# One more drain of GpSimd behind the writes of the last pair but one, in a linear-attention and mixture-of-experts kernel

## The chip, the core and the metric

The kernel runs on one core of a Trainium2 chip. A core has five engines with queues of their own: TensorE (PE in the profile, its weight loads PEld), VectorE (DVE), ScalarE (ACT), GpSimd (POOL) and SyncE (SP). They wait for each other through semaphores. Data moves between the chip's memory and the core by DMA, issued here by SP, by ACT, and, where the rows are picked by a list of indices, by POOL.

The metric is the time of one execution on the device in microseconds (us), as the median of several runs.

## What is computed

Lightning attention over 4 batches, 8 heads, 768 positions and 64 features per head, in blocks of 64 positions, and then a mixture of experts over the 3072 rows of 512 that come out of it. The second part, which the change is about, does this for each row:

```python
for s in range(S):
    fresh_e = int(np.argmax(logits[b, s]))
    if s == 0 or local_gate[b, s] < 0.5:
        e = fresh_e
    else:
        e = prev_e if prev_e >= 0 else fresh_e
    prev_e = e
    ls = logits[b, s] - logits[b, s].max()
    p = np.exp(ls)
    p /= p.sum() + 1e-09
    h = np.maximum(x[b, s] @ w1[e], 0.0)
    out[b, s] = p[e] * (h @ w2[e])
```

There are 8 experts with w1 of 512 x 1024 and w2 of 1024 x 512. Which expert a row goes to is known only while the kernel runs.

## The kernel before

The attention runs first, in 24 steps of 128 positions of one batch. Its rows are written to a buffer in the chip's memory, x_dram. From the logits the kernel works out, on the core itself, tiles of 128 rows that share an expert, and for each slot of a tile the index of its row. A tile is then brought in by an indirect DMA of POOL (`collect`, L725, a gather from x_dram), multiplied by the expert's two weight matrices on TensorE, scaled by the gate, and written by an indirect DMA of POOL to its rows of the output (`scatter`, L768, or `write_pair`, L776).

The first tiles go one by one (L899 to L945). Most of the rest go in pairs of tiles that share an expert (`pair`, L1004). `pair(p)` brings the rows of pair p + 2 and prepares pair p + 1 while it multiplies pair p. How many pairs there are depends on the routing: `rest` (L1272) runs pair 3 and then, by nested branches in `later_pairs` (L1285), as many more as the number `more` says. With these inputs four more run, pairs 4 to 7. Each is a call of `later_pair(k, last)` (L1279). It first writes the result of the pair before it, from the tile `yt`, with `write_pair`: two indirect writes, i = 0 and 1, of 128 rows each, whose indices lie in the small tile `sidxp`. Then it runs its own pair. So when the last pair, 7, begins, pair 6, the last but one, is written. The result of pair 7 goes to another tile (`yl`, which lies in the memory of `s1`, so that the profile calls it s), and is written by the last statement of the kernel, `write_pair(yl)` (L1318).

What sets the order: PE, DVE, SP and ACT run in the order of the code in this part (L1209). POOL's order is left to the scheduler of the framework, within the dependencies. Each engine takes its instructions in turn, and an instruction that waits holds up those behind it on the same engine. The writes to the output don't wait for each other (`apart`, L763). At each join of two branches the framework adds steps that bring the semaphores of the paths to the same counts; POOL's are INC_SWDGE_SEM in the profile and carry the line of the branch or of the end of the program.

The framework closes the program at L1359: SP waits until every DMA has landed, each engine drains, all five meet at a semaphore, POOL clears the semaphores, and they meet again. A drain is an instruction that ends when the engine has finished what was issued to it before.

Of the kernel before, what the change touches and what calls it, by code (L numbers as in the profile page):

```python
# [29 lines left out]
N = B * S  # L30
# [35 lines left out]
def kernel(  # L66
# [9 lines left out]
    nc = tc.nc  # L76
# [313 lines left out]
    sidxp = route.tile([P, 2], U32, name="sidxp")  # L390
# [271 lines left out]
    def rows_out(i):  # L662

        got = nows["got"]
        nc.vector.tensor_scalar(got[:, 0], got[:, 0], 0.0, float(SKIP), ALU.is_equal, ALU.mult)
        nc.vector.tensor_tensor(sidx[i], got[:, 0], gidx[i], ALU.add)

    def both_halves():

        twin = pl[:, :5 * (E + 1)].rearrange("p (k g) -> p k g", k=5)  # L670
        few = nows["few"]
        nc.tensor.matmul(twin[:, :, :E], lhsT=dupb, rhs=few, start=True, stop=True, skip_group_check=True)
        nc.tensor.matmul(twin[:, :, E:], lhsT=dupq, rhs=few[:, :, 0:1], start=True, stop=True, skip_group_check=True)
        got = act.tile([P, 5, E + 1], F32, name="twin", bufs=1)
        nc.vector.tensor_copy(got, twin)
        src = act.tile([P, 2, E + 1], F32, name="srch", bufs=1)
        nc.vector.tensor_scalar(src[:, 0], got[:, 0], -float(P), 0.0, ALU.add, ALU.max)
        nc.vector.tensor_scalar(src[:, 1], got[:, 0], 0.0, float(SKIP), ALU.is_equal, ALU.mult)
        nc.vector.tensor_tensor(src[:, 0], src[:, 0], src[:, 1], ALU.add)
        nc.vector.tensor_tensor(src[:, 0], src[:, 0], got[:, 1], ALU.add)  # L680
        nc.vector.scalar_tensor_tensor(sidxh[:, :E], src[:, 0, :E], 2.0, upper.broadcast_to([P, E]), ALU.mult, ALU.add)
        nc.vector.scalar_tensor_tensor(sidxh[:, E:], src[:, 0, E:], 4.0, fourth, ALU.mult, ALU.add)
        nc.vector.tensor_tensor(got[:, 2], got[:, 2], got[:, 3], ALU.add)
        nc.vector.tensor_tensor(gateh, got[:, 2], got[:, 4], ALU.add)
# [21 lines left out]
    def weights_of(g, i, layers=(1, 2), cond=None, own=None):  # L706
        e = expert(g, own)
        if 1 in layers:
            nc.sync.dma_start(out=w1t[i], in_=w1_src(e), cond=cond, cond_hint=None if cond is None else True)
        if 2 in layers:  # L710
            nc.sync.dma_start(out=w2t[i], in_=w2_src(e), cond=cond, cond_hint=None if cond is None else True)

    def w_of(p):
        return (p + 1) % 2
# [48 lines left out]
    def apart(rows):  # L763

        tc.declare_no_dep(rows.ins, group="out", reason="no row is written twice")
        tc.add_to_no_dep_group("out", rows.ins)
# [9 lines left out]
    def write_pair(y):  # L776

        for i in range(2):
            apart(nc.gpsimd.indirect_dma_start(out=out, out_offset=bass.IndirectOffsetOnAxis(ap=sidxp[:, i:i + 1], axis=0),
                                               in_=y[:, i], in_offset=None, bounds_check=N - 1, oob_is_err=False))  # L780

    def gate_of(g):
        i, j = at(g)
# [6 lines left out]
    def number(k, n):  # L790
        return nc.values_load(arms[k][0:1, 0:1], min_val=0, max_val=n - 1,
                              skip_runtime_bounds_check_because="a number of tiles")
# [15 lines left out]
    with tc.manual_schedule(engines={PE, DVE, SP, POOL}):  # L808
# [71 lines left out]
        yt = act.tile([P, 2, DM], F32, name="y", bufs=1)  # L880
# [70 lines left out]
    def xp(p, j):  # L951
        return xps[2] if j else xps[p % 2]
# [16 lines left out]
    def sums_1(p, ns):  # L969
        fs = sums(s1, a1(p, 0, 0), a1(p, 0, 1), a1(p, 1, 0), a1(p, 1, 1), True)  # L970
        for n in ns:
            fs[n]()
# [21 lines left out]
    def pair_ahead(p):  # L994
        for i in range(2):
            ahead(KA + 2 * p + i, i)

    def pair_flipped(i):
        flipped(xqs[i], xgt[i])

    def pair_moved(p, i):
        moved(xp(p, i), xqs[i])
# [106 lines left out]
    def ahead_half(h):  # L1109
        collect(xgh, 1, G2 - KA + h)  # L1110
# [98 lines left out]
    with tc.manual_schedule(engines={PE, DVE, SP, ACTE}):  # L1209
        more, fulls, halves = (number(k, n) for k, n in enumerate((PMAX - PMIN + 1, E + 1, FIRST_SMALL + 1)))  # L1210
        weights_of(KA, w_of(0), (2,))
        weights_of(G2, 2)
        both_halves()
        pair_ahead(0)
        rows_out(1)
        ahead_half(0)
        sums_1(0, range(3))
        pair_flipped(0)
        pair_flipped(1)
        hidden(0, 0, 0)  # L1220
        hidden(0, 0, 1)
        pair_moved(0, 0)
        moved(xp(0, 1), xqs[1], copy=nc.vector.tensor_copy)
        sums_1(0, (3,))
        output(0, 0)
        sums_of_x(0)
        pair_ahead(1)
        written(4, 0)

        def first_pairs(n, first=2):  # L1230
            hooks = hooks_of_halves(n, first)

            def loads():
                nc.vector.tensor_copy(owner[2], owner[1])
                weights_of(KA + 2, w_of(1), own=2)

            hooks.setdefault(1, []).insert(0, loads)
            pair(0, hooks)
            pair(1, {k - 14: f for k, f in hooks.items()})

        def others():
            weights_of(G1, 2)
            rows = [xgh, *xgt]

            def full_ahead(f):
                collect(rows[f % 3], *at(G1 + f))

            pair(2, {0: [lambda: full_ahead(0)], 10: [lambda: full_ahead(1)], 12: [lambda: full_ahead(2)],
                     6: [lambda: flipped(xqs[0], rows[0])], 7: [lambda: moved(xtt[0], xqs[0])]}, load=False, further=False)

            def w_of_full(f):
                return w_of(2) if f % 2 else 2

            def full(f, n=E):

                i, w = f % 2, w_of_full(f)
                if f + 3 < n:
                    full_ahead(f + 3)
                if not f:
                    weights_of(G1 + 1, w_of_full(1), cond=fulls > 1)  # L1260
                if f + 1 < n:
                    flipped(xqs[1 - i], rows[(f + 1) % 3])
                hidden(i, w, 0)
                hidden(i, w, 1)
                if f + 1 < n:
                    moved(xtt[1 - i], xqs[1 - i])
                output(i, w)
                written(G1 + f, i)
                if f + 2 < n:
                    weights_of(G1 + f + 2, w, cond=fulls > f + 2)  # L1270

            def rest(asked=False):  # L1272
                if not asked:
                    pair_ahead(4)
                weights_of(KA + 8, w_of(4), cond=more > 0)
                rows_of_pair(3)
                pair(3, cond=more > 1, write=False)

                def later_pair(k, last):  # L1279

                    write_pair(yt)
                    pair(PMIN + k, {11: [lambda: rows_of_pair(PMIN + k)]}, next=not last, load=not last and PMIN + k + 2 < PMAX,
                         cond=more > k + 2, write=False)

                def later_pairs(k):  # L1285

                    if PMIN + k + 1 == PMAX:
                        return later_pair(k, True)
                    with tc.If(more > k + 1, preferred_fallthrough_block=True) as cmp:
                        later_pair(k, False)  # L1290
                        later_pairs(k + 1)
                    with cmp.Else():
                        later_pair(k, True)

                with tc.If(more > 0, preferred_fallthrough_block=True) as cmp:
                    later_pairs(0)
                with cmp.Else():
                    for i in range(2):
                        nc.vector.tensor_copy(yl[:, i], yt[:, i])

            with tc.If(fulls == 3, preferred_fallthrough_block=True) as cmp:
                for f in range(3):
                    full(f, 3)
                    if f:
                        ahead(KA + 7 + f, f - 1)
                rest(True)
            with cmp.Else():
                while_more(fulls, 0, E, None, full)
                rest()


        with tc.If(halves == FIRST_SMALL, preferred_fallthrough_block=True, label="halves") as cmp:
            first_pairs(3, 4)
            others()
        with cmp.Else():
            one_of(halves, [3, 4, 2, 5, 1, 6, 0, 7, 8], None, first_pairs)
            others()
        write_pair(yl)  # L1318


# [42 lines left out]
```

## Time and profile before

| what | us |
|---|---|
| median of 3 runs | 442.13 |
| the runs | 440.86, 442.13, 446.67 |
| the profiled execution, its own time | 443.53 |
| its span, first to last instruction | 441.8 |
| PE busy in it | 426.0 |
| POOL busy in it | 109.2 |
| indirect transfers issued by POOL (each about 1.0 us on POOL) | 29 gathers, 27 writes |

The profile is one execution, taken by the hardware profiler. Its times are counted from the first instruction of the span. A row of a group has the line of the kernel, the engine (a q behind it marks its queue: steps that wait, branch or issue and don't count as busy), the operation, the tiles written and read, the count and the times. L1359 is the closing of the program, L779 the indirect write in `write_pair`, L1289 the branch in `later_pairs`. The chain of waits is followed back from the last instruction, at each step to what released it. The granted TensorE clock was 0.996 of full speed on average.

### The profile page before, as it was taken

The page shows a single profiled execution, that of the slowest core. Times are in us where ns is not written, and L with a number is a line of the kernel's source. Part 1 is how long each engine was busy: PE and PEld are TensorE (multiplying, and loading weights), DVE is VectorE, ACT ScalarE, POOL GpSimd, SP SyncE. Part 2 cuts the span into 40 slices and gives each one's busy share as a digit, 9 for nine tenths or more (in the row PEclk, how much of TensorE's full clock was granted, in tenths as well). Part 3 has the DMA queues.
Part 4 walks back from the last instruction along what each step waited for, and adds up shares of the span by engine and source line. Part 5 has one row for each costly group of instructions (what it writes and reads, how often), then busy time and mean ns, then how long its engine had stood idle before and what let it go on. Part 6 is the DMA issues. An engine that isn't in the chain of part 4 may idle for free.

```text
span 441.8 us, 10324 instructions
## 1 busy us (share of the span) xinstructions
PE 426.0 (96%) x4094; PEld 354.7 (80%) x4094; DVE 283.5 (64%) x552; ACT 195.1 (44%) x591; POOL 109.2 (25%) x120
## 2 busy tenths in 40 slices
PE   7998979999999999999999999999999999999993
PEld 7787767787766886977867999667999999898982
DVE  5767886954249868857463784100687879878661
ACT  4245546446455106564234555451555454565110
POOL 4483674430100032114211302100202020020101
PEclk9999999999999999999999999999999999999998
DMA  8999999999999899999993799996165828370101
GB/s 263 412 363 350 329 371 330 330 384 337 370 391 400 300 311 393 401 396 404 395 398 126 266 401 367 336 352 218 40 216 159 310 78 303 122 269 3 55 1 52
DMA packets 48351, 124.84 MB, mean 283 GB/s; under 512 B 3164, under 2 KB 10844, under 8 KB 46368
## 3 DMA queue, kind: packets, MB, share of 16 engines
q1 hardware_dynamic: 42624, 108.03, 66.7%
q0 software_dynamic: 4368, 13.90, 9.0%
q10 hardware_dynamic: 1296, 2.10, 1.3%
q8 instruction: 36, 0.59, 0.5%
q14 instruction: 27, 0.22, 0.1%
HBM read 124.02 MB, written 12.91 MB: 310 GB/s over the span
## 4 chain that ended last, share of the span: by engine, by line
PE 79%; DMA 8%; issue 6%; DVE 6%; POOLq 0%; POOL 0%; DVEq 0%
PE ps L755 13%; PE pk L761 12%; PE ps L986 12%; PE pk L991 11%; DMA out_dram<-y,sidxp 6%; PE po L986 5%; PE po L249 5%; PE pl L991 4%; PE ps L209 3%; PE pr L1147 2%; PE pr L1125 2%; PE po L236 2%; DVE sm L213 2%; PE pk L263 2%; PE ps L201 2%
## 5 line engine op out<-in xcount | busy, mean ns | idle before, releaser
L755 PEld LDWEIGHTS ps<-xt,w 128*128 128x128 f32 x512 | 58.2, 192 | 2.6 <-issue 2.3
L755 PE MATMUL ps<-xt,w 128*128 128x128 f32 x512 | 59.1, 276 | 0.0
L761 PE MATMUL pk<-w,h 128*128 128x512 f32 x128 | 56.5, 593 | 0.0
L761 PEld LDWEIGHTS pk<-w,h 128*128 128x128 f32 x128 | 23.6, 190 | 26.3 <-issue 25.6
L770 POOL DMA_INDIRECT out_dram<-y,sidx x14 | 14.0, 1003 | 105.7 <-DVE y L787 46.5
L727 POOL DMA_INDIRECT xg<-x_dram,gidx x25 | 25.9, 1034 | 54.4 <-DVE lg L741 34.8
L748 ACT COPY xp<-xlast 32x128 f32<-32x128 f32 x128 | 37.8, 296 | 1.7
L213 DVE TENSOR_TENSOR sm<-ps,mask 128x512 f32<-128x512 f32 x46 | 29.5, 682 | 13.5 <-PE ps L209 7.6
L787 DVE TENSOR_SCALAR y<-pk,gate 128x512 f32<-128x512 f32 x8 | 5.9, 744 | 44.8 <-PE pk L761 25.9
L748 ACT COPY xp<-lg 32x128 f32<-32x128 f32 x112 | 33.0, 295 | 2.6
L757 ACT ACTIVATE h<-ps 128x512 f32<-128x512 f32 x16 | 9.6, 597 | 54.8 <-PE ps L755 54.7
L178 POOL TENSOR_TENSOR qd<-inp,lamq 128x512 f32<-128x512 f32 x20 | 25.8, 1289 | 27.9 <-DMA inp<-in_qkv_dram 20.7
L986 PEld LDWEIGHTS ps<-xp,w 128*128 128x128 f32 x256 | 30.5, 192 | 1.6 <-issue 1.3
L986 PE MATMUL ps<-xp,w 128*128 128x128 f32 x256 | 31.3, 275 | 0.0
L986 PE MATMUL ps<-xs,s 128*128 128x128 f32 x256 | 31.2, 275 | 0.0
L991 PE MATMUL pk<-w,h 128*128 128x256 f32 x128 | 30.5, 381 | 0.0
L991 PE MATMUL pk<-s,hsum 128*128 128x256 f32 x128 | 30.3, 380 | 0.0
L986 PEld LDWEIGHTS ps<-xs,s 128*128 128x128 f32 x256 | 29.9, 192 | 0.0
L249 PE MATMUL po<-sm,inp 128*64 128x128 f32 x384 | 27.7, 280 | 1.6 <-issue 0.6
L249 PEld LDWEIGHTS po<-sm,inp 128*64 128x64 f32 x384 | 21.0, 136 | 9.2 <-issue 6.2
L991 PEld LDWEIGHTS pk<-s,hsum 128*128 128x128 f32 x128 | 23.9, 190 | 3.2 <-DVE s L1074 0.2
L991 PEld LDWEIGHTS pk<-w,h 128*128 128x128 f32 x128 | 23.5, 190 | 3.4 <-issue 0.6
(273 smaller groups left out, 779.6 us busy)
## 6 DMA issues: line engine op xcount, KB each, us to landing
w<-in_w_dram SPq DMA_DIRECT2D x43, 2048.0 KB, 12.9
inp<-in_qkv_dram SPq DMA_DIRECT2D x15, 1024.0 KB, 11.5
inp<-in_qkv_dram SPq DMA_DIRECT2D x10, 512.0 KB, 8.1
x_dram<-w SPq DMA_DIRECT2D x12, 256.0 KB, 6.1
inp<-in_qkv_dram SPq DMA_DIRECT2D x4, 768.0 KB, 8.5
x_dram<-xn ACTq DMA_DIRECT2D x8, 256.0 KB, 6.1
w<-in_w_dram SPq DMA_DIRECT2D x4, 512.0 KB, 6.9
x_dram<-inp SPq DMA_DIRECT2D x4, 192.0 KB, 10.5
```

Source lines behind the costliest of these rows:

```text
L178: nc.gpsimd.tensor_tensor(qd, x[:, 0].rearrange("p (a i) -> p a i", i=P), lamq, ALU.mult)
L209: nc.tensor.matmul(ps[u][half, a, first:], lhsT=kt[rows, a, half], rhs=qt[rows, a, first:], start=True, stop=True, skip_group_check=True)
L213: nc.vector.tensor_tensor(sm[:, u], ps[u], mask[:, u], ALU.mult)
L249: nc.tensor.matmul(head(a, u), lhsT=vn[:, a, u], rhs=sm[:, u, a], start=(not c and a < 2), stop=True, skip_group_check=True)
L727: nc.gpsimd.indirect_dma_start(out=xg, out_offset=None, in_=x_dram[:n, :], in_offset=bass.IndirectOffsetOnAxis(ap=gidx[i][:, j:j + 1], axi ...
L748: copy(xt[QP * j:QP * j + QP, :, QP * k:QP * k + QP], blocks[QP * k:QP * k + QP, :, j])
L755: nc.tensor.matmul(ph[:, j], lhsT=w1t[w][:, d, P * f:P * f + P], rhs=xtt[i][:, d], start=(d == 0), stop=(d == DT - 1))
L757: nc.scalar.activation(hq[half, i], ph, ACT.Relu)
L761: nc.tensor.matmul(pys[i], lhsT=hq[f // 4, i][:, f % 4], rhs=w2t[w][:, f], start=(f == 0), stop=(f == FT - 1))
L770: apart(nc.gpsimd.indirect_dma_start(out=out, out_offset=bass.IndirectOffsetOnAxis(ap=sidx[i][:, j:j + 1], axis=0), in_=y, in_offset=None, ...
L986: nc.tensor.matmul(to[:, m], lhsT=a[:, k, P * m:P * m + P], rhs=b[:, k], start=(new and not m and not k), stop=(k == 1), skip_group_check= ...
L991: nc.tensor.matmul(to, lhsT=a[:, f], rhs=b[:, f], start=(new and not f), stop=(f == FT // 2 - 1), skip_group_check=True)
```

## The change

`write_pair` now returns the last of its two writes, and `later_pair`, in the copy of the code that begins the last pair (`last` true), adds one drain of POOL, which the scheduler must place behind that write. The drain has no wait on a semaphore of its own.

```diff
     def write_pair(y):
 
         for i in range(2):
-            apart(nc.gpsimd.indirect_dma_start(out=out, out_offset=bass.IndirectOffsetOnAxis(ap=sidxp[:, i:i + 1], axis=0),
-                                               in_=y[:, i], in_offset=None, bounds_check=N - 1, oob_is_err=False))
+            rows = nc.gpsimd.indirect_dma_start(out=out, out_offset=bass.IndirectOffsetOnAxis(ap=sidxp[:, i:i + 1], axis=0),
+                                                in_=y[:, i], in_offset=None, bounds_check=N - 1, oob_is_err=False)
+            apart(rows)
+        return rows
...
                 def later_pair(k, last):
 
-                    write_pair(yt)
+                    rows = write_pair(yt)
+                    if last:
+                        with tc.issue_after(rows.ins):
+                            nc.gpsimd.drain()
                     pair(PMIN + k, {11: [lambda: rows_of_pair(PMIN + k)]}, next=not last, load=not last and PMIN + k + 2 < PMAX,
                          cond=more > k + 2, write=False)
```

The built program holds 28 such drains, one in each branch that can begin a last pair, and an execution comes through one of them. On all five engines the other instructions stand in the same order as before, with the same waits. On POOL the end of such a branch reads as follows (DMA is an indirect write of 128 rows; ISA is INC_SWDGE_SEM, at the closing's line or at the branch's; a drain is not among the rows that this listing prints):

```order
L1364 ISA
L779 DMA out_dram<-y,sidxp 3072x512
L1364 ISA
L779 DMA out_dram<-y,sidxp 3072x512
L1294 ISA
L1294 UNCONDITIONAL_BRANCH
```

The drain stands right behind the second DMA, ahead of the branch's own semaphore steps and of the ISA at L1294. (The change adds five lines to the file, so that L1359 and L1289 of before are L1364 and L1294 here.)

## The prediction

> **What bounds the kernel now.** I read the page first, then the chain of waits in order of time, then the last 35 us engine by engine, since the change touches only what stands there. The page's busy times say who is full:
>
> ```profile
> PE 426.0 (96%) x4094; PEld 354.7 (80%) x4094; DVE 283.5 (64%) x552; ACT 195.1 (44%) x591; POOL 109.2 (25%) x120
> ```
>
> TensorE is busy for 96% of the span and GpSimd (POOL) for 25%, so until the last matmul nothing that POOL does can matter unless somebody waits for it. After the last matmul it is otherwise. The stretches of the last 82 us show where TensorE stops (the columns are the stretch, its length, and the busy time of PE, PEld, DVE, ACT and POOL):
>
> ```profile
> 410.00:434.00 24.00, 24.00 (x166) 22.46 (x166) 14.09 (x22) 3.33 (x6) 1.40 (x2) 1.00 0.07 26
> 434.00:442.00 8.00, 0.53 (x3) 0.12 (x1) 0.48 (x1) 0.00 (x0) 1.56 (x2) 0.74 0.19 70
> ```
>
> The last 7.3 us hold no matmul. What stands there is the last two row writes and the closing of the program. First POOL's own four last row writes (start, length, what, and in brackets the idle time before and what ended it), then everything that the closing line L1359 issues from 434 us on (engine, operation, count, shortest/median/longest in ns, first and last start in us):
>
> ```profile
> 408.94 1.02 POOL L779 DMA_INDIRECT out_dram<-y,sidxp  x1 [15.07 <-DVE y L1094]
> 411.44 1.00 POOL L779 DMA_INDIRECT out_dram<-y,sidxp  x1 [1.48 <-DVE y L1101]
> 433.60 0.98 POOL L779 DMA_INDIRECT out_dram<-s,sidxp  x1 [21.16 <-DVE s L1094]
> 435.33 0.98 POOL L779 DMA_INDIRECT out_dram<-s,sidxp  x1 [0.74 <-DVE s L1101]
> ```
>
> ```profile
> L1359 SPq EVENT_SEMAPHORE  x14: 17/28/28, 437.3 to 441.8; - x14
> L1359 POOLq EVENT_SEMAPHORE  x4: 17/17/17, 441.0 to 441.7; - x4
> L1359 POOLq DRAIN  x3: 46/113/5865, 435.1 to 441.5; - x3
> L1359 SPq DRAIN  x3: 7/7/7, 438.8 to 441.2; - x3
> L1359 PEldq DRAIN  x2: 13/348/683, 433.9 to 441.3; - x2
> L1359 DVEq DRAIN  x2: 10/40/69, 438.0 to 441.3; - x2
> ```
>
> The first of POOL's drains here starts at 435.1 and lasts 5.865 us, so it ends at 440.97. Only then do the four semaphore steps of POOL (441.0 to 441.7) run, in which all engines meet, and the span ends at 441.8. Everybody else has been ready for long: PE came to its drain at 433.9, DVE at 438.0, SyncE (SP) at 438.8. SP is next to last because it waits for the last two writes to land:
>
> ```profile
> DMA to landing us min/median/max: 2.7/3.2/3.7
> ```
>
> That row is for the two writes from 433 us on. The second, issued at 435.33, has landed 2.7 us later, at 438.1; SP then steps through the rest of its waits up to 438.8. So POOL's drain ends last, some 2.1 us after SP (440.97 - 438.8; this view rounds starts to 0.1), and 2.9 us after the last byte landed. That is the bound at the place of the change.
>
> **What the drain is made of.** The trace has one drain of POOL with row transfers behind it, so its split must be read from its neighbours. One neighbour grows with the number of transfers. INC_SWDGE_SEM, POOL's step that evens the counts of the DMA semaphores between branches, took:
>
> ```profile
> L1359 POOLq INC_SWDGE_SEM  x1: 294/294/294, 176.4 to 176.4; - x1
> L1359 POOLq INC_SWDGE_SEM  x1: 327/327/327, 198.2 to 198.2; - x1
> L1359 POOLq INC_SWDGE_SEM  x1: 508/508/508, 273.8 to 273.8; - x1
> L1359 POOLq INC_SWDGE_SEM  x1: 725/725/725, 393.2 to 393.2; - x1
> ```
>
> How many indirect transfers POOL had issued by then, the gathers (from x_dram) in the first two rows and the writes (to out_dram) in the other two:
>
> ```profile
> 0.00:176.30 176.30, 10.35 (x10) 1.00 0.97 352
> 0.00:393.10 393.10, 29.14 (x29) 1.00 0.86 312
> ...
> 0.00:176.30 176.30, 5.05 (x5) 1.00 0.97 352
> 0.00:393.10 393.10, 25.34 (x23) 1.00 0.86 312
> ```
>
> So 15 transfers before the first and 52 before the last: (725 - 294) / 37 = 11.6 ns for each transfer issued so far, although most of them had landed hundreds of us before. Something is kept for every transfer and nothing clears it while the kernel runs. A drain that clears such a list, entry by entry, would be long at the end (56 transfers) and short right after. Both fit: the two later drains of POOL in the closing took 113 and 46 ns, and the one at the program's start, with no transfer behind it, 184 ns:
>
> ```profile
> L1355 POOLq DRAIN  x1: 184/184/184, 0.4 to 0.4; - x1
> ```
>
> **The change, part by part.** It adds one executed drain on POOL, without a wait on a semaphore, behind the write at 411.44. It removes nothing and moves nothing on the other engines.
>
> The added drain. From below it costs 0.18 us (the drain at the start), from above what the last one took, 5.87 us. I take about 5.7 us (54 of 56 entries). Behind it on POOL stand one INC_SWDGE_SEM, a branch, and the writes of the last pair. In the chain of waits these are:
>
> ```profile
> 412.61 0.11 POOLq L1289
> 412.72 0.04 issue
> 412.76 0.04 POOLq L1289
> 412.80 2.58 issue
> 415.38 0.03 POOLq L779
> 415.41 0.05 issue
> 415.46 0.02 POOLq L779
> 415.47 17.89 issue
> 433.37 0.03 POOLq L779
> ```
>
> INC_SWDGE_SEM ends at 412.72. POOL is through its branch at 412.80, spends 2.58 us on getting to the next code, and from 415.47 waits 17.9 us for the last pair's result. A drain of 5.7 us that starts near 411.4 moves all of this to some 420. It lies beside the waiting, so it costs nothing; were that cover gone it would cost what it lasts beyond the write. Nobody else waits for POOL in this stretch: the result tile of the last pair is another one (s, not y), and what DVE overwrites is the index tile sidxp, late and behind transfers that were issued before the drain:
>
> ```profile
> 431.51 0.16 DVE L774 COPY sidxp<-sidx 128x2 uint32<-128x2 uint32 x1
> ```
>
> The last drain. It now has 2 transfers behind it and 54 entries less. From below the relief is 54 x 11.6 ns = 0.6 us (the growth of INC_SWDGE_SEM); from above 54/56 of all 5.87 us, 5.7 us. The 2.9 us that the drain ran past the last landing are nearest to what is asked, because there nothing was left to wait for: shared over 56 transfers they are 52 ns each, and 54 x 52 ns = 2.8 us. So I expect the drain to end within about 0.1 us of the landing, by 438.2.
>
> What is late next is SP: ready at 438.8, set by the landing of the last write, which the change does not touch. From 2.1 us on, relief buys nothing. The sum: 2.1 us less in the span, 441.8 to 439.7. The profiled execution took 443.53 us by its own clock, 1.7 us outside the span, and becomes 441.4. It stood 1.4 us above the median of the three runs, 442.13, so the median becomes 440.0.
>
> **A rule against it.** The drains of SP, DVE and PE in the closing take 7 to 13 ns, but for two of 69 and 683 ns that come first on their engine. The Trainium skill, VectorE: DVE Perf Modes, section The DRAIN you can't avoid, says that the drains of a program's beginning and end are a constant of some 12 ns on all five engines. By that rule the added drain costs 12 ns, the last one has nothing to give up, and the sum is 442.1, the time of rival 1 below. For most drains of the other engines the trace agrees; the row of 5.865 us speaks against it on POOL.
>
> **The rivals.**
> 1. The drain is a fixed delay after the last landing, or after the last transfer, whatever came earlier; its 2.9 us past the landing then stay. For it: one sample cannot tell 2.9 us fixed from 56 x 52 ns, and a second drain would be short either way. Against it: the growing INC_SWDGE_SEM, and that INC_SWDGE_SEM behind the write at 411.44 was done at 412.72, so POOL's cores had no long tail after a transfer. Time: 442.1.
> 2. Only part is per transfer, down to the 11.6 ns of INC_SWDGE_SEM. Then 0.6 us go, and any price under 2.1 us / 54 = 39 ns leaves POOL last. Time: 441.5 at that end, less as the price nears 39 ns.
> 3. Slower: the added drain holds POOL's queue beyond 433.37, because it waits for more than the row transfers. It would have to last from 411.4 to 412.7 and then the 17.9 us of waiting, 19 us in all, three times the longest drain seen; each us beyond that is a us of time. At twice that, 38 us, the time is 461. Nothing in the trace speaks for it: the last weight load moves no data after 410 (DMA share 0.07).
>
> **How the numbers follow.** The forecast (full relief, SP last) gets 0.60, rival 1 gets 0.21, rival 2 gets 0.15, rival 3 gets 0.04. The time is that of the forecast, 440.0. The range goes from 440.0 less 1.3 (the lowest run stood 1.3 below the median) to 442.1 of rival 1 plus as much: 438.7 to 443.4. Two per cent, 8.8 us, is about what a measurement of this kernel tells from no change; the whole last drain is 5.9 us, so faster by that much gets 0.01, slower 0.02 (half of rival 3), within it 0.97.
>
> **What the profile would show.** If I am right, a drain of several us stands on POOL from 411 on, to some 417, POOL's next move comes near 420 and its write still at 433.6; the last drain is under 3.2 us long, and the closing steps start near 438.9, just after SP, instead of 441.0. INC_SWDGE_SEM behind the added drain would be near 0.12 us (0.294 less 15 x 0.0116). I am wrong if the added drain is short, or if the last one still ends after 440.

## The result and the profile after

The changed kernel took 441.68 us (median of 22 runs, 439.46 to 444.92), the kernel before 443.73 us over as many runs (440.86 to 446.67); the medians differ by 2.05 us. The ratio that is estimated from all these runs is 0.9949, with a 95% interval from 0.9926 to 0.9972: 2.3 us less, between 1.2 and 3.3. By the bound of 2% that is no change; by its interval it is a small gain, and 2.1 us was the forecast.

The closing line, L1364 in the changed file, in the profile after, from 430 us on (engine, operation, count, shortest/median/longest in ns, first and last start in us):

```profile
L1364 SPq EVENT_SEMAPHORE  x14: 17/28/28, 438.8 to 440.9; - x14
L1364 POOLq EVENT_SEMAPHORE  x4: 17/17/17, 440.1 to 440.9; - x4
L1364 POOLq DRAIN  x3: 46/113/3127, 436.4 to 440.7; - x3
L1364 SPq DRAIN  x3: 7/7/7, 440.1 to 440.4; - x3
```

The last drain went from 5.865 to 3.127 us. It starts at 436.4 and ends at 439.5; SP comes to its drains at 440.1, and the meeting steps of POOL start at 440.1 too, right behind SP. The two have changed places: POOL was last, now SP is. The added drain, and the last four writes of POOL in the same profile:

```profile
L1286 POOLq DRAIN  x1: 5711/5711/5711, 412.5 to 412.5; - x1
```

```profile
410.20 1.01 POOL L779 DMA_INDIRECT out_dram<-y,sidxp  x1 [15.06 <-DVE y L1096]
412.70 1.00 POOL L779 DMA_INDIRECT out_dram<-y,sidxp  x1 [1.48 <-DVE y L1103]
434.87 0.98 POOL L779 DMA_INDIRECT out_dram<-s,sidxp  x1 [21.17 <-DVE s L1096]
436.59 0.98 POOL L779 DMA_INDIRECT out_dram<-s,sidxp  x1 [0.74 <-DVE s L1103]
```

It lasts 5.711 us, nearly as long as the last one did before (5.865). The chain of waits shows that it was paid out of waiting time (start, length, what):

```profile
418.68 0.05 POOLq L1294
418.73 2.56 issue
421.29 0.03 POOLq L779
421.32 0.05 issue
421.37 0.02 POOLq L779
421.38 13.25 issue
434.63 0.03 POOLq L779
```

Before, POOL was at this place from 415.47 on and waited 17.9 us; now it comes at 421.38 and waits 13.25 us. The writes still start when VectorE is done (0.74 us of idle time ahead of the last write in both).

The spans, 441.8 and 441.0, differ by only 0.8 us, because this execution was already 1.3 us later at the write of 410.20 (408.94 before), ahead of the added drain. From the start of the last write to the end of the span it is 6.5 us before (441.8 - 435.33) and 4.4 us after (441.0 - 436.59): 2.1 us.

### The profile page after: what moved, and what is told of

Its sections match the earlier page's. It is cut to its first block, busy times and chain, and to the rows that moved or that the text cites. A ratio compares the mean times of both kernels' runs of the same rounds, so it can differ in the third digit from the quotient of the medians.

```text
span 441.0 us, 10325 instructions
## 1 busy us (share of the span) xinstructions
PE 425.8 (97%) x4094; PEld 354.2 (80%) x4094; DVE 284.6 (65%) x552; ACT 195.0 (44%) x591; POOL 109.3 (25%) x120
## 4 chain that ended last, share of the span: by engine, by line
PE 73%; DMA 15%; issue 5%; DVE 4%; POOL 1%; POOLq 0%; ACT 0%; SPq 0%
PE ps L755 13%; PE pk L761 13%; PE ps L988 12%; PE pk L993 11%; DMA out_dram<-y,sidxp 7%; DMA inp<-in_qkv_dram 7%; PE po L988 5%; PE pl L993 4%; PE po L249 3%; PE pr L1149 2%; PE pr L1127 2%; PE ps L209 2%; DVE sm L213 1%; DMA lamb<-in_lam_dram 1%; PE po L236 1%
## 5 line engine op out<-in xcount | busy, mean ns | idle before, releaser
L761 PEld LDWEIGHTS pk<-w,h 128*128 128x128 f32 x128 | 23.6, 190 | 26.3 <-issue 25.6
L240 ACT ACTIVATE kv<-kv,lamq 128x64 f32<-128x64 f32 x64 | 17.1, 337 | 20.7 <-PE po L236 20.7
```

Of the source, the lines that this page charges most:

```text
L240: nc.scalar.mul(kv[:, a], kv[:, a], lamq[:, a, P - 1:P])
L761: nc.tensor.matmul(pys[i], lhsT=hq[f // 4, i][:, f % 4], rhs=w2t[w][:, f], start=(f == 0), stop=(f == FT - 1))
```

## The experiments

After the result, three accounts of a drain's length were open. Theory 1: it works through the transfers since the drain before, 83 ns each, and is over at the earliest at the landing of the last one (the last drain before ended 4.65 us after the end of the last write on POOL: 56 x 83 ns). Theory 2: it waits for that landing and then works through them, 51 ns each (it ended 2.88 us after the landing: 56 x 51 ns). The third, that the length goes with something else (bytes, rows, the time since the start), is tested with them. The two drains of the one profile, with 54 transfers and with 2, cannot tell theories 1 and 2 apart, so the number of transfers had to be varied.

**The changed kernel once more** (`again`).

> The changed kernel once more, beside the others on one chip. Theory 1 (backlog with a floor): a drain of POOL ends at the later of two times, the end of the last transfer on POOL plus 83 ns for each transfer since the drain before, and the landing of the last transfer plus 0.1 us. From it: the added drain ends 54 x 0.083 = 4.48 us after the end of the write ahead of it, the last one 0.1 us after the landing, the time 2.1 us under before. Theory 2 (walk after the landing): a drain ends at the landing plus 51 ns for each transfer. It gives the same last drain, 0.1 us after the landing. This run cannot tell the two apart at the end of the program.

Measured: ratio to before 0.9968 [0.9944, 0.9991], 1.4 us less (0.4 to 2.5). The added drain ended 4.48 us after the end of the write ahead of it, to the nanosecond as in the first profile, though that write landed 2.18 us after its end on POOL here and 1.76 us there (by the last of the 16 steps of its semaphore in the trace). Theory 2 would have had the drain 0.4 us longer here. The last drain ended 0.11 us after the landing.

The last write landed later too, by SP's step 2.20 us after its end on POOL against 1.80 us in the first profile, and SP waits for it. So the stretch from that end to the end of the span is 3.79 us here, 3.39 us in the first profile and 5.51 us before: the relief at the end is 1.7 us in this profile and 2.1 us in the first.

**A drain three pairs earlier** (`drain_14`). 14 transfers are left for the last drain. The edit, against the changed kernel:

```diff
-                    if last:
+                    if not k:
                         with tc.issue_after(rows.ins):
                             nc.gpsimd.drain()
```

> The drain moved three pairs ahead, behind the writes of pair 3, so that 14 transfers stand between it and the last drain. Theory 1: 14 x 83 ns = 1.16 us after the last write's end on POOL, which is before the landing (1.8 us after that end); so the last drain ends 0.1 us after the landing, and the time is that of the changed kernel, 2.1 us under before. Theory 2: 14 x 51 ns = 0.71 us after the landing, 0.6 us later than in the changed kernel; SP is ready 0.75 us after the landing, so the time hardly moves, but the last drain is 0.6 us longer (3.7 against 3.1 us).

Measured: 0.9963 [0.9937, 0.9988], 1.6 us less (0.5 to 2.8), the same gain as in `again` on the same chip. The last drain was neither theory's:

```profile
L1364 SPq EVENT_SEMAPHORE  x13: 17/28/28, 438.2 to 439.7; - x13
L1364 POOLq EVENT_SEMAPHORE  x4: 17/17/17, 439.0 to 439.7; - x4
L1364 POOLq DRAIN  x3: 46/113/3574, 435.2 to 439.5; - x3
```

It ends at 438.80, 0.60 us after the landing as SP sees it (438.20): half a microsecond too late for theory 1, 0.1 us too early for theory 2.

**Twenty more transfers, small and plain** (`small_20`), added to the kernel before; they carry 16 rows of 16 bytes each and nothing reads them.

```diff
+    junk = const.tile([16, 20, 4], F32, name="junk")
+
+    def small(js):
+        for j in js:
+            nc.gpsimd.dma_start(out=junk[:, j], in_=wg[:16, 0, :4])
...
         finished(0)
+        small(range(8))
         weights(2)
...
         finished(1)
+        small(range(8, 20))
         weights(3)
```

> No added drain, but 20 more transfers of POOL, plain ones of 16 rows of 16 bytes, in POOL's quiet time at about 120 to 150 us: 76 transfers for the last drain. If every transfer counts alike, theory 1 gives a drain that ends 76 x 83 ns = 6.31 us after the last write's end on POOL, theory 2 the landing (1.8 us) and 76 x 51 ns = 3.88 us, 5.7 us. The time is 1.7 or 1.0 us over before. If rows or bytes count and not transfers, or the time since the program began, the drain ends 4.65 us (at most 4.9 us) after the last write, as before, and the time does not move.

Measured: 1.0056 [1.0035, 1.0078], 2.5 us more (1.6 to 3.5).

```profile
435.91 0.98 POOL L785 DMA_INDIRECT out_dram<-s,sidxp  x1 [21.20 <-DVE s L1102]
437.64 0.98 POOL L785 DMA_INDIRECT out_dram<-s,sidxp  x1 [0.74 <-DVE s L1109]
```

```profile
L1367 POOLq DRAIN  x3: 46/109/7508, 437.4 to 445.5; - x3
L1367 SPq DRAIN  x3: 7/7/7, 441.5 to 445.2; - x3
```

The drain ends at 444.91, 6.29 us after the last write's end on POOL (438.62), against 6.31 by theory 1. A plain transfer of 256 bytes counts like an indirect one of 128 rows: neither bytes, rows nor elapsed time explain it. Theory 2 was put at 5.7 us, but with the landing of this profile, 2.32 us after the write's end, it gives 6.2 us, so this run alone does not rule it out. From the last write's end to the end of the span it is 7.13 us against 5.51 before, 1.6 us more. That is the lower end of the interval; the runs do not show what else the 20 transfers cost.

**One drain, between the last two writes** (`between`), where POOL has nothing to hide it behind. The edit is against the kernel before:

```diff
-    def write_pair(y):
+    def write_pair(y, end=False):
...
+            apart(rows)
+            if end and not i:
+                with tc.issue_after(rows.ins):
+                    nc.gpsimd.drain()
...
-        write_pair(yl)
+        write_pair(yl, True)
```

> One drain, not behind the writes of the last pair but one but between the two writes of the last pair, where POOL has no waiting to hide it. Theory 1: it ends 55 x 83 ns = 4.57 us after the first write's end on POOL, the second write starts 4.1 us later than in the changed kernel, the last drain ends 0.1 us after its landing: 2.0 us over before. Theory 2: the first write lands 2.8 us after its end on POOL, the drain ends 55 x 51 ns = 2.8 us after that, 5.6 us after the write, the time 3.0 us over before. If a drain were free (a rival), the time would be that of the changed kernel.

Measured: 1.009 [1.0059, 1.0122], 4.0 us more (2.6 to 5.4), more than either theory, though the interval holds the 3.0 us of theory 2. The profile decides:

```profile
L784 POOLq DRAIN  x1: 6499/6499/6499, 433.7 to 433.7; - x1
```

```profile
433.97 0.98 POOL L779 DMA_INDIRECT out_dram<-s,sidxp  x1 [21.43 <-DVE s L1098]
441.11 0.98 POOL L779 DMA_INDIRECT out_dram<-s,sidxp  x1 [6.15 <-issue]
```

The drain ends at 440.24, 5.28 us after the first write's end on POOL (theory 1: 4.57, theory 2: 5.6, or 5.8 with the landing of this profile) and 2.28 us after its landing (437.96). POOL then takes another 0.87 us to the next write. So a drain is not free, and where it is not covered it costs more than it saves.

**Theory 3.** 0.60 us after the landing with 14 transfers, 2.28 us with 55: that is 43 and 41.4 ns for each transfer, about half of theory 1's 83 ns. So a drain seems to go through the transfers twice, and the second pass begins only when the last transfer has landed. With E the end of the last transfer on POOL, L its landing and N the transfers since the drain before, the end is the later of E + N x 41.5 ns and L, plus N x 41.5 ns. That was put to three more kernels, with the expectations on record before they ran.

**21 transfers left** (`drain_21`): the added drain moved behind the write of the first full tile. In this run and the next, `scatter` and `written` also return the write (not shown), and the drain of the changed kernel is taken out.

```diff
-                written(G1 + f, i)
+                done = written(G1 + f, i)
+                if not f:
+                    with tc.issue_after(done.ins):
+                        nc.gpsimd.drain()
...
-                    if last:
-                        with tc.issue_after(rows.ins):
-                            nc.gpsimd.drain()
```

> The drain stands behind the write of the first full tile, so that 21 transfers are left for the last drain. Theory 3 (from the runs so far): a drain goes twice through the transfers since the drain before, 41.5 ns for each and time, and the second pass begins only when the last transfer has landed. With E the end of the last transfer on POOL, L its landing and N the transfers, it ends at the later of E + N x 41.5 ns and L, plus N x 41.5 ns. Here N x 41.5 ns = 0.87 us, so it ends 0.87 us after the landing as SP sees it. Theory 1: 21 x 83 ns = 1.74 us after E, which is about L, so 0.1 us after the landing at most. Theory 2: 21 x 51 ns = 1.07 us after the landing. SP is ready 0.75 us after the landing, so by theory 3 the time is 0.1 to 0.2 us over that of the changed kernel, 1.9 us under before.

Measured: 0.9933 [0.9901, 0.9964], 3.0 us less (1.6 to 4.4). The profile of `drain_21`:

```profile
L1366 SPq EVENT_SEMAPHORE  x13: 17/28/28, 442.5 to 444.2; - x13
L1366 POOLq EVENT_SEMAPHORE  x4: 17/17/17, 443.5 to 444.2; - x4
L1366 POOLq DRAIN  x3: 46/113/4319, 439.1 to 444.0; - x3
L1366 SPq DRAIN  x3: 7/7/7, 443.2 to 443.7; - x3
```

Landing at 442.55, drain's end at 443.43: 0.89 us against 0.87 by theory 3, 0.1 by theory 1, 1.07 by theory 2. POOL is last again, by 0.14 us (SP is ready at 443.30).

**41 transfers left** (`drain_41`): the added drain behind the write of tile 4, ahead of all pairs.

```diff
-        written(4, 0)
+        with tc.issue_after(written(4, 0).ins):
+            nc.gpsimd.drain()
...
-                    if last:
-                        with tc.issue_after(rows.ins):
-                            nc.gpsimd.drain()
```

> The drain stands behind the write of tile 4, ahead of the pairs, so that 41 transfers are left for the last drain. Theory 3: the last drain ends 41 x 41.5 ns = 1.70 us after the landing (first pass done before it). Theory 1: 41 x 83 ns = 3.40 us after the last write's end on POOL, which is 1.2 to 1.7 us after a landing that comes 1.75 to 2.2 us after that end. Theory 2: 41 x 51 ns = 2.09 us after the landing. By theory 3 the closing starts 1.70 - 0.75 = 0.95 us later than in the changed kernel, so 1.2 us of the 2.1 are left, if the drain costs nothing at its own place. There POOL has no long wait: behind it stand the loads of the loop counts and the gather of a later pair, while weights are being loaded; its 15 transfers take two passes of 0.6 us and the wait for a landing of 4 to 8 us, and if somebody waits for that gather the time is up to 5 us longer.

Measured: 0.9986 [0.9952, 1.0019], 0.6 us less (2.1 less to 0.8 more).

```profile
437.99 0.98 POOL L781 DMA_INDIRECT out_dram<-s,sidxp  x1 [0.75 <-DVE s L1105]
```

```profile
L1364 SPq EVENT_SEMAPHORE  x11: 27/28/28, 440.9 to 441.6; - x11
L1364 SPq DRAIN  x2: 7/7/7, 441.6 to 441.7; - x2
L1364 POOLq DRAIN  x1: 4882/4882/4882, 437.8 to 437.8; - x1
```

Landing at 440.93, drain's end at 442.64: 1.70 us, as theory 3 had it (theory 1 with this landing: 1.44, theory 2: 2.09). The closing starts 1.0 us after SP is ready. The expected 1.2 us of gain lie within the interval, but so does none, so this run's time says nothing on what the early drain costs at its own place. The traces do. These are the write ahead of it, the gather behind it and the next write, before and in `drain_41`:

```profile
175.15 1.01 POOL L770 DMA_INDIRECT out_dram<-y,sidx  x1 [5.90 <-DVE y L787]
177.48 1.03 POOL L727 DMA_INDIRECT xg<-x_dram,gidx  x1 [1.32 <-DMA out_dram<-y,sidx]
198.31 1.75 POOL L1153 DMA_INDIRECT out_dram<-yh,sidxh  x1 [8.84 <-DVE yh L1152]
```

```profile
177.72 1.02 POOL L770 DMA_INDIRECT out_dram<-y,sidx  x1 [5.90 <-DVE y L791]
186.87 1.11 POOL L727 DMA_INDIRECT xg<-x_dram,gidx  x1 [8.13 <-DMA xg<-x_dram,gidx]
200.87 1.74 POOL L1157 DMA_INDIRECT out_dram<-yh,sidxh  x1 [8.84 <-DMA out_dram<-y,sidx]
```

The gather comes 9.2 us behind the write in place of 2.3, but the next write is 2.56 us later than before, where the one ahead of the drain was 2.57 us later already. The delay that had been feared (up to 5 us) did not come.

**A drain in every later pair** (`drain_each`).

```diff
-                    if last:
-                        with tc.issue_after(rows.ins):
-                            nc.gpsimd.drain()
+                    with tc.issue_after(rows.ins):
+                        nc.gpsimd.drain()
```

> A drain behind the writes of every pair from 3 on, four executed drains in place of one. Theory 3: the first has 42 transfers behind it, the next three 4 each, the last one of the program 2, which ends 0.1 us after the landing as in the changed kernel. Each drain in between lasts until its write has landed (2 to 7 us) and holds back the gather behind it by as much, but that gather's rows are needed some 18 us later; so the time is that of the changed kernel. If the held gathers matter (a rival), it is over it by 1 us or more.

Measured: 0.995 [0.992, 0.9979], 2.2 us less (0.9 to 3.6), the gain of one drain.

```profile
L1285 POOLq DRAIN  x4: 3256/7877/9158, 334.7 to 408.7; - x4
```

Three of the four are 7.5 to 9.2 us long, most of it waiting for a landing that comes 6.0 to 6.9 us after the write's end on POOL (1.8 us in the fourth). The gather behind the first drain comes 9.83 us after the write (344.76 against 334.93), before it came 1.31 us after it (338.78 against 337.47). The first writes of successive pairs still follow each other at 24.66 us, as before, so the held gathers cost nothing.

The last drains of seven of the profiles and the two added drains near the end, from the unrounded records (us; E, L and N as above, L as SP's step for the last write begins):

| drain | N | end - E | end - L | theory 3 |
|---|---|---|---|---|
| before, the last | 56 | 4.65 | 2.88 | E + 4.65 |
| after, the added one | 54 | 4.48 | | E + 4.48 |
| small_20, the last | 76 | 6.29 | 3.98 | E + 6.31 |
| between, the added one | 55 | 5.28 | 2.28 | L + 2.28 |
| drain_41, the last | 41 | 3.67 | 1.70 | L + 1.70 |
| drain_21, the last | 21 | 3.10 | 0.89 | L + 0.87 |
| drain_14, the last | 14 | 2.36 | 0.60 | L + 0.58 |
| after, the last | 2 | 1.91 | 0.11 | L + 0.08 |
| between, the last | 1 | 1.83 | 0.07 | L + 0.04 |

In the first three the first pass, by the law, outlasts the landing, in the others the landing comes later. One law holds for 1 to 76 transfers within 0.03 us.

Seven of the added drains stand earlier in the program, where no step of SP marks the landing. Their landings can be read from the last of the 16 steps of the write's semaphore. All seven landings come after the first pass:

| added drain | N | L - E | end - L | theory 3 |
|---|---|---|---|---|
| drain_14 | 42 | 6.11 | 1.76 | L + 1.74 |
| drain_21 | 35 | 7.47 | 1.48 | L + 1.45 |
| drain_41 | 15 | 5.01 | 0.66 | L + 0.62 |
| drain_each, first | 42 | 6.17 | 1.76 | L + 1.74 |
| drain_each, second | 4 | 6.86 | 0.21 | L + 0.17 |
| drain_each, third | 4 | 6.03 | 0.21 | L + 0.17 |
| drain_each, fourth | 4 | 1.82 | 0.21 | L + 0.17 |

The law holds there too, within 0.05 us, though the landing came up to 7.5 us after E. What follows the landing is thus measured by itself; the 41.5 ns ahead of it are the rest of the 83 ns, seen only where the landing comes first. What POOL does in the two passes no run shows; only the counts and the times are shown.

## Why the prediction was right

*What bounds the end.* Right. POOL's last drain ended last before, and SP ends last after. The relief is cut off at SP: 2.1 us by the tail of the two profiles, 2.3 us (1.2 to 3.3) by the runs. One size in that step hung on the execution that was read. SP is ready 0.75 us after the last landing, and over the nine profiles that landing came 1.75 to 2.3 us after the write's end on POOL (1.77 us in the profile before). By the same sum the relief goes from 2.2 down to 1.6 us, so 2.1 us is near its upper end.

*The added drain lies beside waiting.* Right, also in size: 5.7 us was taken, 5.711 measured, and 13.25 us of waiting remain. `between` shows the other half of that step, the price without the cover: 4.0 us more than before in place of 2.3 less. The 461 us of rival 3 for a drain of 38 us adds 19 us to the kernel before; on the forecast of 440.0, which keeps the relief at the end, it would be 459.

*The last drain ends within about 0.1 us of the landing.* Right: 0.11 us in the two profiles of the changed kernel.

*52 ns for each transfer, read from the 2.9 us after the landing.* The mechanism, work that goes with the transfers, was right; this term was mis-sized. It is 83 ns, in two passes of 41.5 ns, and the first pass runs while the last write is still under way. By this law the first pass of the kernel before ended at 438.63, after the landing at 438.08, so the transfers alone set the length. Counting from the landing left out the work done ahead of it. The sum did not suffer, since any price over 39 ns brings POOL below SP, and the end within 0.1 us of the landing does not test the size, since two transfers cost little at 52 or at 83 ns; the price mattered for where the drain may stand.

*The list is cleared by a drain.* Right, and seen in the neighbour that the prediction used. In `drain_41`, right behind the early drain, the two steps of INC_SWDGE_SEM that took 294 and 288 ns before now take:

```profile
L1364 POOLq INC_SWDGE_SEM  x2: 118/120/123, 185.9 to 186.7; - x2
```

The prediction had put 0.12 us on the step behind the added drain, at the branch. That one took 0.184 us, half as much again. The step at the branch has another price than those the prediction had read: 1.269 us before with 54 transfers, 0.979 with 39 (`drain_41`), 0.579 with 19 (`drain_21`) and 0.439 with 12 (`drain_14`), some 20 ns for each transfer in place of 11.6.

*The rivals.* The fixed delay (0.21) falls with the profile after: same landing, 2.7 us less drain. So does the small price for each transfer (0.15): 83 ns are above the 39 ns at which POOL stays last. The added drain that holds up the queue (0.04) did not come about at the place of the change. The rule of the Trainium skill (VectorE: DVE Perf Modes, The DRAIN you can't avoid), a constant of some 12 ns on all five engines, does not hold for POOL here: the first drain of the closing, with transfers behind it, took 3.0 to 7.5 us in these runs, and those of the start and the closing with none behind them 0.05 to 0.18 us. The added drains, which that section does not speak of, took 3.3 to 10.2 us.

*The absolute time.* 440.0 was forecast and 441.68 measured, inside the range. The difference is the base: the three runs shown beforehand had a median of 442.13, all 22 have one of 443.73.

## What to carry to other kernels

GpSimd's drain at the end of this kernel was paid for every DMA that GpSimd had issued since its last drain: with 83 ns each, 56 of them made 4.65 us after the last write, of which some 2 us lay beyond what everybody else needed. One more drain in a stretch where GpSimd waits anyway takes those 2 us off, and it may stand well ahead of the end: by an estimate from the table, with up to (0.75 - 0.03) / 0.0415 = 17 transfers behind it the last drain here stays hidden behind SyncE's own wait for the landing. With 14 it did (`drain_14`), with 21 it ended 0.14 us too late (`drain_21`). Look first at what is late next, since the gain stops there, and at what stands behind the drain on its engine, since it holds that back until the last transfer has landed and the second pass is done (6.9 to 10.2 us for six of the added drains here; no later write of POOL was late for it).

## What the runs showed of the hardware that was not expected

- A drain of GpSimd behaves like two passes of 41.5 ns for each transfer since the drain before, the second not before the landing of the last transfer (all 19 profiled drains with 1 to 76 transfers, within 0.05 us). A plain transfer of 256 bytes counts as much as an indirect one of 128 rows of 2 KB.
- The price of INC_SWDGE_SEM, too, goes with the transfers since the last drain and starts anew after one (294 to 118 ns at the same step).
- Drains of 7.5 to 9.2 us in the middle of the pairs (`drain_each`), each holding back a gather, left no trace in the time: the pairs kept their 24.66 us.
